# A fused kernel whose engines follow a planned order: weight blocks of 1024 columns, a backward run that hands out banks, and one more unit turned by TensorE

## The chip, the cores and the metric

The kernel runs on one core of one Trainium2 chip. The metric is device time in microseconds (us), the median of several executions of the same program. TensorE (PE) does the matrix products, VectorE (DVE) and ScalarE (ACT) the elementwise work, GpSimd (POOL) almost nothing here, and SyncE (SP) issues every DMA from one queue in program order.

## The reference, cut to what matters

```python
# attention: q, k, v, a_re, a_im of shape (4, 8, 768, 48); a normalised to at most 0.999 in size
for t in range(S):
    new_re = ar * S_re - ai * S_im
    new_im = ar * S_im + ai * S_re
    S_re, S_im = new_re + k[t] (x) v[t], new_im
    y[:, :, t] = q[t] . S_re
x = y.transpose(0, 2, 1, 3).reshape(3072, 384)
h = x @ w_in                                    # layer 1: 384 -> 2048
g = 0 if h <= -1, h if h >= 1, else (h + 1) ** 2 / 4
x = g @ w_out                                   # 2048 -> 384
x = x / sqrt(mean(x * x) + 1e-6) * rms_g        # layer 2
out = (silu(x @ w_gate) * (x @ w_val)) @ w_out2 # 384 -> 1536 -> 384
```

The weights lie in DRAM as 64-bit floats.

## The kernel before, in words

**Units.** The work is cut into 12 units: 2 pairs of batches times 6 chunks of 128 time steps, so that a unit is 256 tokens. A unit goes through attention (`attn`), layer 1 (`moe1`) and layer 2 (`moe2`). Units 0 and 1 go through layer 1 in two halves of 128 tokens.

**Attention of a unit.** A long chain on DVE (tiles X, pr, C, K, E) multiplies up the decays. At its end the real part is X minus the part `a<-X,E`. Either DVE subtracts (`X<-a`, called the fold here), or, for a unit in `PEW['add']`, TensorE adds the two while it transposes (`onto_tokens`). The decays then scale q and k on the token side (`factors`). q and k are split into two f16 parts (`qhi`, `qlo`, `khi`, `klo`), and each part is transposed by a DMA, or for a unit in `PEW['t']` by products with `nid` (minus the identity) that ACT takes out of PSUM (`turned`, L738). For a unit in `PEW['k']` the low part of k comes from a product on TensorE instead of a DVE subtraction (`low_pe`, L747). For a unit in `PEW['n']` TensorE also turns the normalised tokens between the layers (`xnh`, `xnl` from tiles `nh`, `nl`).

**Weights.** `split_w` (L772) loads a block of 64-bit weights, DVE rebuilds an f32 word by one TENSOR_SCALAR and two SCALAR_TENSOR_TENSOR (tile `wv` for layer 1, `spt` for gate and value), ACT writes the f16 high part, and TensorE and ACT make the low part in pieces of 384 columns (two products and one ACT copy each). The blocks of `w_in` and `w_out` pass through slots cut out of tiles that layer 2 fills later (`ring1` for the loads, `ringc` for the words). All weights then stay on the chip.

**The order.** No loop sets the order of the instructions. All operations are recorded, class `Plan` makes a list schedule from a table of costs (`order`), and the program is issued in that order from one line (`issue`), so every row of the trace has line L456. The priority of an operation is its `late`, the latest time by a backward run (`latest`) through the schedule before, plus a shift that the table `SHIFT` gives for its stage. Attention of the next units is recorded between the steps of the layers at `RATES`. `bank` (6 PSUM banks) and `tmp` (4 tiles) are handed out while `order` runs, within the `CAPS` of each kind of user. The backward run does not know of them.

**Stretches.** In the trace before, the first layer-1 product of unit 0 starts at 90.35 us, the first layer-2 (gate) product at 200.77 us, and the first layer-1 product of unit 2 at 296.50 us. From 373 us on the products follow each other almost without a gap, up to 1056.5 us.

Of the kernel before, what the change touches and what calls it, by code (L numbers as in the profile page):

```python
# [48 lines left out]
PEW = {'add': [1], 'sum': [], 'k': [2], 'q': [], 'p': [], 'g': [], 'm': [], 't': [0], 'x': [], 'n': []}  # L49

SHIFT = {'w1a': 12, 'm23': 12, 't40': -12, 'm22': 2, 'w2': 25, 't30': -1, 'c2': 3, 'y21': 5, 'c3': -1}
ORDER = [(1, 0), (1, 1), (2, 0), (2, 1), (1, 2)]
RATES = [14.7, 0, 40.2, 27.7, 29.4]
RATE = 0.62
AHEAD1, STEP1, STEP2 = 4, 5, 6
LAG = 3
CHECKS = 12
# [3 lines left out]
CAPS = {'mo': 4, 'at': 4, 'w': 4, 'n': 2, 'mo_': 3, 'at_': 3, 'w_': 2, 'out_': 1, 'one_': 1}  # L61
ROUNDS = 1
# [20 lines left out]
class Plan:  # L83
# [92 lines left out]
    def add(self, variants):  # L176
# [19 lines left out]
        if "T" in variants:  # L196
            f32 = args[1].dtype == F32
            mm = (300 if name == "transpose" else 6 + n * (4 if f32 else 1), kw_rows(args, kw))
# [56 lines left out]
    def cost(key, name, n, args, kw, ins):  # L255
# [13 lines left out]
        if key == "T":  # L269
            f32 = args[1].dtype == F32  # L270
            return 0.4167e-3 * (300 if name == "transpose" else 6 + n * (4 if f32 else 1))
# [27 lines left out]
    def latest(self, res):  # L299
# [6 lines left out]
        ready = [0.0] * len(ops)  # L306
        free = {k: 0.0 for k in self.engines}
        wait_q = {k: [] for k in self.engines}
        av_q = {k: [] for k in self.engines}
        eng = [next(iter(op.alts)) for op in ops]  # L310
        for op in ops:
            if not left[op.idx]:
                heapq.heappush(wait_q[eng[op.idx]], (0.0, op.idx))
        n = 0
        while n < len(ops):
# [15 lines left out]
            op = ops[heapq.heappop(a)[1]]  # L331
# [4 lines left out]
            op.late = -st  # L336
            for p in op.preds:
# [5 lines left out]
        for op in ops:  # L343
            op.late -= first

# [10 lines left out]
    def order(self):  # L356
# [22 lines left out]
        while len(res) < len(ops):  # L379
# [25 lines left out]
            lack = [v[0] for v in new if not spare[v[0]]] + [v[3] for v in new if turns.get(v[3], 0) != v[4] or using.get(v[3], 0) >= CAPS[v[3]]]  # L405
# [261 lines left out]
def fused_kernel(ctx, tc, q, k, v, a_re, a_im, w_in, w_out, w_gate, w_val, w_out2, rms_g, out, a_ch, qvk_t, given=None):  # L667
# [95 lines left out]
    ring1 = itertools.cycle([flat16(w2)[:, i * 3072:(i + 1) * 3072].bitcast(I64) for i in range(3)])  # L763
    ring12 = itertools.cycle([flat16(w2)[:, i * 3072:(i + 1) * 3072].bitcast(I64) for i in range(2)])
    diag = [flat16(w2)[:, 6144 + i * 256:6400 + i * 256].bitcast(F32) for i in range(KD)]
    ringc = itertools.cycle([flat16(wv)[:, i * 1536:(i + 1) * 1536].bitcast(F32) for i in range(6)])
# [5 lines left out]
    def split_w(src, hi, lo, n, scale, phase, dg=None, part=""):  # L772
# [18 lines left out]
        for c0 in range(0, n, 384):  # L791
            sl = slice(c0, min(n, c0 + 384))
# [11 lines left out]
    def w_1_steps():  # L804
        for f in range(0, DFF, 512):
            sl = slice(f, min(DFF, f + 512))
            for kc in range(KD):
                split_w(w_in[kc * P:(kc + 1) * P, sl], wi_h[:, kc, sl], wi_l[:, kc, sl], sl.stop - f, SW, 1, part="abcd"[f // 512])
                yield
            for j in range(f // P, f // P + 4, 2):  # L810
# [640 lines left out]
```

## Time and profile before

| | us |
|---|---|
| median of 3 executions | 1066.04 (1065.69 to 1067.02) |
| profiled execution, its own time | 1067.5 |
| its span in the profile | 1065.8 |
| PE busy | 995.5 |
| DVE busy | 817.2 |
| ACT busy | 812.7 |

The profile shows one execution. Its span starts with the first and ends with the last instruction, and lies 1.7 us under that execution's own time. An engine counts as busy while at least one of its instructions runs, and the granted clock is the share of its full speed that TensorE was given.

### The profile page before, as it was taken

The numbers are of one execution on the slowest core, as the hardware profiler recorded it, in microseconds if no ns is written. First come the engines' busy times: TensorE is split into PE (matmuls) and PEld (weight loads), VectorE is DVE, ScalarE is ACT, GpSimd is POOL, SyncE is SP. The second block draws the span as 40 slices with busy tenths as digits, with TensorE's granted clock in tenths as the row PEclk, the third lists the DMA queues.
The fourth block names the chain that finished last, engine by engine and source line by source line (L and its number), as shares of the span: only waits on it lengthen the run. The fifth ranks groups of instructions, "written<-read, shape, count | busy, mean of one in ns | idle before, by whom it ended". The sixth has DMA issues, their size and how long they took to land.

```text
span 1065.8 us, 23000 instructions
## 1 busy us (share of the span) xinstructions
PE 995.5 (93%) x9224; PEld 775.2 (73%) x9224; DVE 817.2 (77%) x1721; ACT 812.7 (76%) x1585; POOL 16.7 (2%) x27
## 2 busy tenths in 40 slices
PE   3577998998997899999999999999999999999996
PEld 1355866876875688778777787787887787877874
DVE  9989889979869889698797697896996984633321
ACT  6469879867787798899877897978978989946221
POOL 2000000000000000000000000000000000000000
PEclk9878998999998999999999999999999999999999
DMA  7563265256444443444335526336444321210000
GB/s 255 193 208 121 48 192 138 73 148 159 130 105 123 118 126 94 138 107 105 103 90 147 141 62 168 84 102 169 108 132 139 78 73 36 48 24 16 16 9 26
DMA packets 156018, 115.87 MB, mean 109 GB/s; under 512 B 135296, under 2 KB 138368, under 8 KB 155904
## 3 DMA queue, kind: packets, MB, share of 16 engines
q1 hardware_dynamic: 155904, 114.33, 40.0%
q8 instruction: 74, 1.21, 0.4%
q14 instruction: 40, 0.33, 0.1%
HBM read 77.07 MB, written 4.72 MB: 77 GB/s over the span
## 4 chain that ended last, share of the span: by engine, by line
PE 68%; DVE 16%; ACT 7%; DMA 4%; issue 4%; POOL 0%; SPq 0%; DVEq 0%; ACTq 0%
PE bank L456 43%; PE acc L456 25%; DVE tmp L456 3%; DVE X L456 3%; DVE pr L456 2%; ACT tmp L456 2%; DVE wv L456 2%; DMA w<-in_moe_w_out_dram 1%; ACT L456 1%; DMA spt<-in_moe_w_in_dram 1%; DVE gml L456 1%; DMA qvk<-in_qvk_t_dram 1%; ACT S L456 1%; DVE a L456 1%; ACT X L456 1%
## 5 line engine op out<-in xcount | busy, mean ns | idle before, releaser
L456 DVE SCALAR_TENSOR_TENSOR tmp<-bank,tmp 128x512 f32<-128x512 f32 (+1 forms) x184 | 117.0, 639 | 102.9 <-ACT tmp L456 56.2
L456 PEld LDWEIGHTS <-gmh 128*128 128x128 f16 x1344 | 130.1, 98 | 76.4 <-issue 10.6
L456 PE MATMUL bank<-xTh,wi_h 128*128 128x256 f16 (+1 forms) x672 | 169.1, 262 | 5.2 <-DVE S L456 2.6
L456 PE MATMUL bank<-xTl,wi_h 128*128 128x256 f16 (+1 forms) x672 | 169.0, 262 | 0.3 <-DMA xTl<-nl 0.3
L456 PE MATMUL bank<-xTh,wi_l 128*128 128x256 f16 (+1 forms) x672 | 169.0, 262 | 0.0
L456 ACT ACTIVATE gmh<-tmp 128x512 f16<-128x512 f32 (+1 forms) x184 | 107.5, 588 | 64.7 <-DVE tmp L456 50.4
L456 PE MATMUL bank<-xnh,wv 128*128 128x256 f16 x864 | 155.2, 273 | 0.0
L456 PEld LDWEIGHTS <-wi_h 128*128 128x128 f16 x1344 | 127.2, 100 | 27.1 <-issue 5.8
L456 PE MATMUL acc<-w,gmh 128*128 128x384 f16 x576 | 140.6, 326 | 1.9 <-DVE nl L456 0.7
L456 PEld LDWEIGHTS <-wv 128*128 128x128 f16 x1296 | 126.5, 98 | 16.7 <-issue 0.7
L456 PE MATMUL acc<-wo_h,gmh 128*128 128x384 f16 x384 | 126.5, 329 | 3.6 <-ACT tmp L456 3.6
L456 PE MATMUL acc<-wo_h,gml 128*128 128x384 f16 x384 | 126.3, 329 | 1.8 <-DVE gml L456 1.8
L456 PE MATMUL acc<-wo_l,gmh 128*128 128x384 f16 x384 | 126.5, 329 | 0.0
L456 ACT ACTIVATE tmp<-tmp 128x512 f32<-128x512 f32 (+1 forms) x224 | 124.7, 565 | 2.1
L456 PE MATMUL bank<-xnl,wv 128*128 128x256 f16 x432 | 117.7, 273 | 0.0
L456 PE MATMUL bank<-xnh,wg_l 128*128 128x256 f16 x432 | 117.7, 273 | 0.0
L456 PE MATMUL bank<-xnl,wg_h 128*128 128x256 f16 x432 | 117.7, 273 | 0.0
L456 PE MATMUL bank<-xnh,wg_h 128*128 128x256 f16 x432 | 117.7, 273 | 0.0
L456 PEld LDWEIGHTS <-gml 128*128 128x128 f16 x672 | 66.0, 98 | 47.5 <-DVE gml L456 2.6
L456 PEld LDWEIGHTS <-wg_h 128*128 128x128 f16 x864 | 84.1, 98 | 16.1 <-issue 1.1
L456 PE MATMUL acc<-w,gml 128*128 128x384 f16 x288 | 93.9, 326 | 0.0
L456 ACT ACT_TABLE_LOAD x67 | 86.0, 1283 | 4.9 <-DMA spt<-in_moe_w_in_dram 3.0
(185 smaller groups left out, 2192.1 us busy)
## 6 DMA issues: line engine op xcount, KB each, us to landing
qvk<-in_qvk_t_dram SPq DMA_DIRECT2D x24, 576.0 KB
spt<-in_moe_w_out_dram SPq DMA_DIRECT2D x14, 768.0 KB
a<-in_a_ch_dram SPq DMA_DIRECT2D x12, 768.0 KB
w<-in_moe_w_in_dram SPq DMA_DIRECT2D x12, 512.0 KB
w<-in_moe_w_out_dram SPq DMA_DIRECT2D x8, 768.0 KB
w<-in_moe_w_gate_dram SPq DMA_DIRECT2D x6, 768.0 KB
w<-in_moe_w_val_dram SPq DMA_DIRECT2D x6, 768.0 KB
spt<-in_moe_w_out_dram SPq DMA_DIRECT2D x12, 384.0 KB
```

Of the source, the lines that this page charges most:

```text
L456: getattr(self.engines[k], name)(*args, **kw)
```

## The change

Five things change together.

- `w_in` is loaded and decoded in blocks of 1024 columns instead of 512, so there are 6 loads of 1 MB instead of 12 of 512 KB. A slot grows with them: `ring1` has 2 slots instead of 3, `ringc` 4 instead of 6. The pieces for the low part are 512 columns wide where the block allows it.
- The backward run `latest` hands out banks and tiles too, within the same caps, and the two runs are repeated up to 10 times (`ROUNDS`) instead of once.
- `PEW`: unit 1's fold goes from TensorE to DVE (`'add'`), the low part of unit 2's k from TensorE to DVE (`'k'`), unit 1's q and k are turned by TensorE and not by DMA (`'t'`), and so are the normalised tokens of unit 0 (`'n'`).
- The tables that set priorities and the pace of the side work are new: `SHIFT` has 43 entries instead of 9, and `RATES`, `RATE`, `STEP2`, `CHECKS` and `CAPS` differ.
- The planner's price of a transpose rises from 300 to 320 columns, and a product costs at least 61.

```diff
-PEW = {'add': [1], 'sum': [], 'k': [2], 'q': [], 'p': [], 'g': [], 'm': [], 't': [0], 'x': [], 'n': []}
-SHIFT = {'w1a': 12, 'm23': 12, 't40': -12, 'm22': 2, 'w2': 25, 't30': -1, 'c2': 3, 'y21': 5, 'c3': -1}
+PEW = {'add': [], 'sum': [], 'k': [], 'q': [], 'p': [], 'g': [], 'm': [], 't': [0, 1], 'x': [], 'n': [0]}
+SHIFT = {'t11': 10, 'c0': -52, 'w1h': 416, 'w1e': 5, 't20': 9, 't10': 19, 't40': -45, 'y10': -108, 't21': -6, 'y20': 4, 'w3c': -46, 'y21': -156, 'y31': -154, 'm13': 61, 'w1a': -33, 't00': -24, 'c1': 9, 'y00': 1, 'y01': -103, 'm20': 3, 't01': -24, 'y11': -35, 'c5': -37, 'w1b': -7, 'c4': 10, 'm10': 7, 'w3a': 8, 'm11': 5, 'c2': -138, 'y40': 44, 'm12': 72, 'y30': 28, 'm21': 27, 'w3b': -61, 'w1g': 137, 'w2': -101, 't41': -178, 'y41': -20, 'w1f': -5, 't31': -12, 'm22': 8, 't30': -2, 'c3': 8, 'w2b': -6}
 ORDER = [(1, 0), (1, 1), (2, 0), (2, 1), (1, 2)]
-RATES = [14.7, 0, 40.2, 27.7, 29.4]
-RATE = 0.62
-AHEAD1, STEP1, STEP2 = 4, 5, 6
+RATES = [11.7, 0, 19.2, 44.7, 47.4]
+RATE = 0.58
+AHEAD1, STEP1, STEP2 = 4, 5, 12
...
-CHECKS = 12
+CHECKS = 10
...
-CAPS = {'mo': 4, 'at': 4, 'w': 4, 'n': 2, 'mo_': 3, 'at_': 3, 'w_': 2, 'out_': 1, 'one_': 1}
-ROUNDS = 1
+CAPS = {'mo': 4, 'at': 4, 'w': 4, 'n': 2, 'mo_': 3, 'at_': 2, 'w_': 1, 'out_': 1, 'one_': 1}
+ROUNDS = 10
 LAT = {'V': 0.13, 'A': 0.145, 'G': 0.1, 'T': 0.0, 'S': 0.0}
 XLAT = {'V': 0.13, 'A': 0.145, 'G': 0.1, 'T': 0.2, 'S': 0.0}
...
         mm = None
         if "T" in variants:
...
-            mm = (300 if name == "transpose" else 6 + n * (4 if f32 else 1), kw_rows(args, kw))
+            mm = (320 if name == "transpose" else max(61, 6 + n * (4 if f32 else 1)), kw_rows(args, kw))
...
             return 0.06 + n * {"tensor_tensor": 2.12e-3, "scalar_tensor_tensor": 3.75e-3, "memset": 1.1e-3}.get(name, 3.6e-3)
         if key == "T":
...
-            return 0.4167e-3 * (300 if name == "transpose" else 6 + n * (4 if f32 else 1))
+            return 0.4167e-3 * (320 if name == "transpose" else max(61, 6 + n * (4 if f32 else 1)))
         return 1.25 if "transpose" in name else 0.4
...
             prio[i] = t + ops[i].alts[k]
         left = [len(op.succs) for op in ops]
         ready = [0.0] * len(ops)
+        eng = [next(iter(op.alts)) for op in ops]
         free = {k: 0.0 for k in self.engines}
         wait_q = {k: [] for k in self.engines}
         av_q = {k: [] for k in self.engines}
-        eng = [next(iter(op.alts)) for op in ops]
+        users, spare, held, stuck, turns, using = {}, {}, set(), {}, {}, {}
         for op in ops:
+            for v in op.tiles:
+                users[v] = users.get(v, 0) + 1
+                spare.setdefault(v[0], [0.0] * v[2])
+                turns[v[3]] = max(turns.get(v[3], 0), v[4])
             if not left[op.idx]:
                 heapq.heappush(wait_q[eng[op.idx]], (0.0, op.idx))
         n = 0
...
                 heapq.heappush(a, (-prio[i], i))
             if not a:
                 continue
-            op = ops[heapq.heappop(a)[1]]
+            i = heapq.heappop(a)[1]
+            op = ops[i]
+            new = [v for v in op.tiles if v not in held]
+            lack = self.lacking(new, spare, turns, using)
+            if lack:
+                stuck.setdefault(lack[0], []).append(i)
+                continue
+            when = max([spare[v[0]][0] for v in new], default=0.0)
+            if when > t + 1e-9:
+                heapq.heappush(w, (when, i))
+                continue
+            for v in new:
+                held.add(v)
+                heapq.heappop(spare[v[0]])
+                turns[v[3]], using[v[3]] = v[4] - 1, using.get(v[3], 0) + 1
+                for j in stuck.pop(v[3], ()):
+                    heapq.heappush(wait_q[eng[j]], (max(ready[j], t), j))
             n += 1
             c = op.alts[k]
             st = t + (op.dma + 2.0 if op.dma else 0.0) + c
             free[k] = t + max(op.dma, c) if op.dma else st
             op.late = -st
+            for v in op.tiles:
+                users[v] -= 1
+                if not users[v]:
+                    heapq.heappush(spare[v[0]], st + XLAT[k])
+                    using[v[3]] -= 1
+                    for j in stuck.pop(v[0], []) + stuck.pop(v[3], []):
+                        heapq.heappush(wait_q[eng[j]], (max(ready[j], st + XLAT[k]), j))
             for p in op.preds:
                 ready[p] = max(ready[p], st + (LAT[eng[p]] if eng[p] == k else XLAT[eng[p]]))
                 left[p] -= 1
...
         first = min(op.late for op in ops)
         for op in ops:
             op.late -= first
+    @staticmethod
+    def lacking(new, spare, turns, using):
+        return ([v[0] for v in new if not spare[v[0]]] +
+                [v[3] for v in new if turns.get(v[3], 0) != v[4] or using.get(v[3], 0) >= CAPS[v[3]]])
...
                 late, i = heapq.heappop(a)
             op = ops[i]
             new = [v for v in op.tiles if v not in held]
-            lack = [v[0] for v in new if not spare[v[0]]] + [v[3] for v in new if turns.get(v[3], 0) != v[4] or using.get(v[3], 0) >= CAPS[v[3]]]
+            lack = self.lacking(new, spare, turns, using)
             if lack:
                 stuck.setdefault(lack[0], []).append(i)
                 continue
...
     flat16 = lambda t: t.rearrange("p two a b -> p (two a b)")
-    ring1 = itertools.cycle([flat16(w2)[:, i * 3072:(i + 1) * 3072].bitcast(I64) for i in range(3)])
+    ring1 = itertools.cycle([flat16(w2)[:, i * 4096:(i + 1) * 4096].bitcast(I64) for i in range(2)])
     ring12 = itertools.cycle([flat16(w2)[:, i * 3072:(i + 1) * 3072].bitcast(I64) for i in range(2)])
...
-    ringc = itertools.cycle([flat16(wv)[:, i * 1536:(i + 1) * 1536].bitcast(F32) for i in range(6)])
+    ringc = itertools.cycle([flat16(wv)[:, i * 2048:(i + 1) * 2048].bitcast(F32) for i in range(4)])
     spt = plan.tile(mp, [P, 768], I64, "spt")
...
         flat = lambda t: t.rearrange("p a b -> p (a b)") if len(t.shape) > 2 else t
         hf, lf = flat(hi), flat(lo)
-        for c0 in range(0, n, 384):
-            sl = slice(c0, min(n, c0 + 384))
+        step = 512 if n % 512 == 0 else 384
+        for c0 in range(0, n, step):
+            sl = slice(c0, min(n, c0 + step))
             w = sl.stop - c0
             lp = bank("w")[:, 0:w]
             with plan.group():
...
         return src[j * P:(j + n) * P, :].rearrange("(a p) c -> p a c", p=P)
     def w_1_steps():
-        for f in range(0, DFF, 512):
-            sl = slice(f, min(DFF, f + 512))
+        for f in range(0, DFF, 1024):
+            sl = slice(f, f + 1024)
             for kc in range(KD):
-                split_w(w_in[kc * P:(kc + 1) * P, sl], wi_h[:, kc, sl], wi_l[:, kc, sl], sl.stop - f, SW, 1, part="abcd"[f // 512])
+                split_w(w_in[kc * P:(kc + 1) * P, sl], wi_h[:, kc, sl], wi_l[:, kc, sl], sl.stop - f, SW, 1, part="ab"[f // 1024])
                 yield
-            for j in range(f // P, f // P + 4, 2):
-                split_w(rows(w_out, j, 2), wo_h[:, j:j + 2, :], wo_l[:, j:j + 2, :], 2 * DM, SW, 1, part="efgh"[f // 512])
+            for j in range(f // P, f // P + 8, 2):
+                split_w(rows(w_out, j, 2), wo_h[:, j:j + 2, :], wo_l[:, j:j + 2, :], 2 * DM, SW, 1, part="efgh"[j // 4])
                 yield
...
```

Counted over the whole program, TensorE gains 64 products that turn q and k and 12 that turn `nh` and `nl`, and loses the 12 products of the fold with `a` (its 12 with `X` become plain transposes), the products for unit 2's k, and some of the pieces of weights. On DVE 18 instructions of `wv` go (TENSOR_SCALAR 20 to 14, SCALAR_TENSOR_TENSOR 40 to 28), `a<-X,E` goes from 23 to 24, `X<-a` from 22 to 24, `klo` from 22 to 24, and the one `X<-X,E` goes. ACT gains 16 copies of turned q and k and 4 of turned tokens and loses 6 of high parts and 12 of low parts of weights and 4 of `klo`; its table loads go from 67 to 71. SP issues 306 DMAs instead of 324.

**The start of SP's queue.** `w_0` is the slot tile of the weights, `a_0` the decays, `qvk` the tokens. Before, the program begins:

```order
L456 DMA a_0_104<-in_a_ch_dram 128x1536
L456 DMA w_0_74<-in_moe_w_in_dram 128x512 x2
L456 DMA qvk_113<-in_qvk_t_dram 128x1152
L456 DMA w_0_74<-in_moe_w_in_dram 128x512
L456 DMA qvk_114<-in_qvk_t_dram 128x1152
L456 DMA g_s_75<-in_moe_rms_g_dram 128x3x1
L456 DMA w_0_74<-in_moe_w_out_dram 128x2x384 x2
L456 DMA w_0_74<-in_moe_w_in_dram 128x512 x2
L456 DMA w_0_74<-in_moe_w_out_dram 128x2x384
```

With the change:

```order
L490 DMA a_0_104<-in_a_ch_dram 128x1536
L490 DMA w_0_74<-in_moe_w_in_dram 128x1024 x2
L490 DMA qvk_113<-in_qvk_t_dram 128x1152
L490 DMA qvk_114<-in_qvk_t_dram 128x1152
L490 DMA g_s_75<-in_moe_rms_g_dram 128x3x1
L490 DMA w_0_74<-in_moe_w_in_dram 128x1024
L490 DMA w_0_74<-in_moe_w_out_dram 128x2x384 x4
L490 DMA w_0_74<-in_moe_w_in_dram 128x1024 x3
```

Two large loads now stand where three smaller ones stood before a slot is used again, and the third load of `w_in` is the first that has to wait for a slot.

**PE where unit 1's fold is.** `idt` is the identity, `xTh` and `wi_h`, `wi_l` are layer 1's tokens and weights of unit 0, `gmh` and `wo_h` the second product of layer 1. Before:

```order
L456 MATMUL bank_119<-xTh_99,wi_l_68 128x128
L456 MATMUL bank_103<-idt_81,X_105 128x128 x6
L456 MATMUL bank_122<-idt_81,a_0_104 128x128 x6
L456 LDWEIGHTS gmh_154
L456 MATMUL acc_0_158<-wo_h_69,gmh_154 128x384
```

With the change:

```order
L490 MATMUL bank_119<-xTh_99,wi_l_68 128x128
L490 MATMUL bank_123<-spt_92,w_0_74 128x384
L490 LDWEIGHTS nid_80
L490 MATMUL bank_123<-wv_73,nid_80 128x384
L490 MATMUL bank_115<-idt_81,X_105 128x128 x3
L490 MATMUL bank_116<-idt_81,X_105 128x128 x3
L490 LDWEIGHTS wi_h_67
```

Twelve products with `X` and `a` became six plain transposes of `X` alone, and a piece of the gate weights (`spt`) now stands ahead of them.

**DVE where the gate and value weights are decoded.** `spt` holds the decoded word, one TENSOR_SCALAR and two SCALAR_TENSOR_TENSOR to a block. Before, the eleventh of the 12 blocks stands amid the norm of unit 0 (`y_1`) and unit 2's chain (X, pr):

```order
L456 TENSOR_TENSOR y_1_165<-y_1_164 128x1
L456 TENSOR_TENSOR X_105<-pr_106 128x2x96
L456 TENSOR_TENSOR y_1_165<-y_1_165,ms_163 128x1
L456 TENSOR_SCALAR spt_92<-w_0_74 128x768
L456 TENSOR_SCALAR y_1_165<-y_1_165 128x1
L456 TENSOR_TENSOR pr_106<-X_105 128x384
L456 TENSOR_TENSOR y_1_165<-y_1_165,y_1_164 128x1
L456 SCALAR_TENSOR_TENSOR spt_92<-w_0_74,spt_92 128x768
```

With the change it stands amid the masks of unit 1's scores (`tmp<-bank,maskt`) and some 80 rows earlier:

```order
L490 TENSOR_TENSOR pl_127<-tmp_148,ph_126 128x512
L490 TENSOR_TENSOR pl_130<-tmp_128,ph_129 128x512
L490 SCALAR_TENSOR_TENSOR spt_92<-w_0_74,spt_92 128x768
L490 TENSOR_SCALAR spt_92<-w_0_74 128x768
L490 SCALAR_TENSOR_TENSOR spt_92<-w_0_74,spt_92 128x768
L490 SCALAR_TENSOR_TENSOR h_0_0_134<-bank_119,h_0_0_134 128x384
L490 TENSOR_SCALAR fx_133<-St_88 128x1
```

In number of instructions the stretch of DVE ahead of the first gate product is nearly unchanged (415 before, 419 after), but it holds more of the long ones: `a<-X,E` 6 instead of 3, `X<-a` 6 instead of 2, no `X<-X,E` instead of 1 (unit 2's fold now stands ahead of the gate product too), a twelfth block of gate and value weights, and two blocks of `w_out2`. Ahead of the first layer-1 product DVE has 151 instructions instead of 169: the 18 of `wv` are gone and the rest is the same.

## Rows read from the trace of the kernel before

**Rows 1.** Page, section 1: busy time, share of the span and instructions of each engine.
```profile
PE 995.5 (93%) x9224; PEld 775.2 (73%) x9224; DVE 817.2 (77%) x1721; ACT 812.7 (76%) x1585; POOL 16.7 (2%) x27
```

**Rows 2.** Stretches: length; busy PE, PEld, DVE, ACT, POOL; granted clock, DMA share, GB/s.
```profile
0.00:90.35 90.35, 50.92 (x245) 30.11 (x245) 83.75 (x172) 56.50 (x119) 6.49 (x13) 0.83 0.61 205
90.35:200.77 110.42, 102.13 (x1144) 82.64 (x1142) 101.07 (x250) 92.60 (x229) 2.21 (x3) 0.95 0.44 117
200.77:296.50 95.73, 92.40 (x815) 70.80 (x813) 82.46 (x179) 72.49 (x136) 0.79 (x1) 1.00 0.53 139
296.50:373.00 76.50, 67.55 (x618) 49.98 (x616) 60.83 (x126) 58.74 (x116) 0.70 (x1) 0.93 0.45 116
373.00:1056.50 683.50, 682.33 (x6409) 541.57 (x6407) 488.17 (x995) 531.75 (x987) 6.51 (x9) 1.00 0.35 91
```

**Rows 3.** What PE waited for, 201 to 374 us: total, times, longest.
```profile
PE acc L456 <- ACT tmp L456: 4.3, 2, 3.6
PE bank L456 <- DVE X L456: 2.2, 1, 2.2
PE bank L456 <- DVE pl L456: 1.9, 2, 1.2
PE acc L456 <- DVE gml L456: 1.8, 1, 1.8
```

**Rows 4.** DVE groups by form, whole span: count, busy and mean ns, idle before.
```profile
L456 DVE SCALAR_TENSOR_TENSOR wv<-w,wv 128x512 uint32<-128x512 uint32 x24 | 16.5, 689 | 0.0
L456 DVE SCALAR_TENSOR_TENSOR wv<-w,wv 128x768 uint32<-128x768 uint32 x16 | 15.2, 956 | 0.0
L456 DVE TENSOR_TENSOR a<-X,E 128x1536 f32<-128x1536 f32 x23 | 40.2, 1749 | 0.0
L456 DVE TENSOR_TENSOR X<-a 128x768 f32<-128x768 f32 x22 | 20.9, 948 | 0.0
```

**Rows 5.** What DVE waited for, 0 to 90.35 us: total, times, longest.
```profile
DVE wv L456 <- DMA w<-in_moe_w_out_dram: 3.5, 2, 2.1
DVE wv L456 <- DMA w<-in_moe_w_in_dram: 0.6, 1, 0.6
```

**Rows 6.** Chain that ended last, two loads on it: start, length, what.
```profile
40.65 6.56 DMA w<-in_moe_w_out_dram
64.20 7.74 DMA w<-in_moe_w_out_dram
```

**Rows 7.** PE in order of time, unit 1's fold on TensorE, one batch.
```profile
119.49 2.91 PE L456 MATMUL bank<-idt,X 128*128 128x128 f32 x12
...
124.91 0.33 PE L456 MATMUL acc<-wo_h,gmh 128*128 128x384 f16 x1
```

**Rows 8.** PE in order of time, six plain transposes (unit 0) and what follows.
```profile
78.86 1.06 PE L456 MATMUL bank<-idt,X 128*128 128x128 f32 x6
79.76 0.19 PE L456 MATMUL bank<-vh,ph 128*128 128x48 f16 x1
```

**Rows 9.** PE in order of time, low part of unit 2's k, one batch.
```profile
217.40 0.81 PE L456 MATMUL bank<-S,idt 128*128 128x384 f32 x2
...
219.02 0.27 PE L456 MATMUL bank<-xnh,wg_h 128*128 128x256 f16 x1
```

**Rows 10.** PE in order of time, eight turns of unit 0 and what follows.
```profile
95.79 0.65 PE L456 MATMUL bank<-nid,klo 128*96 128x128 f16 x8 [0.55 <-DVE klo L456]
96.27 0.22 PE L456 MATMUL bank<-xTh,wi_h 128*128 128x128 f16 x1
```

**Rows 11.** ACT groups by form, whole span.
```profile
L456 ACT ACT_TABLE_LOAD x67 | 86.0, 1283 | 4.9 <-DMA spt<-in_moe_w_in_dram 3.0 <-PEq L1423 0.8
L456 ACT ACTIVATE khT<-bank 96x512 f16<-96x512 f32 x4 | 2.1, 580 | 0.0
```

**Rows 12.** ACT in order of time, around one table load.
```profile
209.35 1.28 ACT L456 ACT_TABLE_LOAD   x1
210.65 0.62 ACT L456 ACTIVATE S<-S,e 128x384 f32<-128x384 f32 x1
```

## The prediction, made before the changed kernel had run

> **What bounds the kernel now.** I read the busy shares first. PE is busy 995.5 us, DVE 817.2 and ACT 812.7 [rows 1], which says that PE leads and not where. So I cut the span into stretches at PE's own milestones [rows 2]. From 373 to 1056.5 us PE is busy 682.33 of 683.50 us at the full clock, 2.4 GHz: there only PE's own work counts, and what DVE, ACT or a DMA do is hidden. Before 90 us PE is busy 50.92 of 90.35 us and DVE 83.75: the start is DVE's. From 90 to 201 us DVE is busy 101.07 of 110.42, PE 102.13 and ACT 92.60: all three are nearly full, and DVE has the chains that the others wait for. From 201 to 373 us PE is busy 92.40 + 67.55 of 172.23 us, so 12.3 us idle, and the granted clock of the second half is 0.93. At 1.2 GHz a product takes twice as long, so (1 - 0.93) x 76.5 = 5.4 us is the most that the lower clock can have cost there. Then I asked what PE waited for in that stretch [rows 3]: ACT's `tmp` 4.3 us, and DVE's `X`, `pl` and `gml` 2.2 + 1.9 + 1.8 = 5.9 us. The 9.3 us from 1056.5 to the end of the span stay as they are, since the same instructions end both programs.
>
> The time is thus the moment at which the first gate product can start (200.8 us), plus the PE work that is left then, plus the stalls among it, plus the tail. I cost the change in these four parts.
>
> **The start, up to the first layer-1 product: -1 us.** The list of DVE instructions ahead of it is the same but for 18 fewer of `wv`. A SCALAR_TENSOR_TENSOR takes 689 ns at 512 columns and 956 at 768 [rows 4], so 256 columns more cost 267 ns and 1024 columns some 1223 (an estimate from these two). Two blocks of 512 at 689 cost 1378, so each pair that is merged saves 155 ns, and 18 merged pairs, the TENSOR_SCALAR put in at the same price, 2.8 us at most. At least it is nothing, if DVE then waits for something else. I take 1.5. Against it stands the smaller number of slots. DVE waits 3.5 + 0.6 = 4.1 us for weights now [rows 5]. Two loads of `w_out` on the critical chain took 6.56 and 7.74 us of 768 KB [rows 6], a mean of 7.2; scaled by bytes, 1 MB would take 9.5 (an estimate; with two in flight instead of three it may be less). With the decode behind it, about 3 us for a block of 1024 and 2.5 for one of 768, a slot turns in 12.5 or 9.7 us. Two slots have 6 large and 8 small loads to turn: (6 x 12.5 + 8 x 9.7) / 2 = 76 us of the 90. They fit, though with only 14 us over, where three slots had far more. Bounds: the 4.1 us go altogether, or each of the 12 loads that use a slot again is late by 1 us more, +12. I take +0.5, nearer the low end because of the 14 us over.
>
> **From there to the first gate product: +9 us.** The new order brings more DVE work ahead of it in nearly the same number of instructions. The folds: 3 more `a<-X,E` at 1749 ns and 4 more `X<-a` at 948, less one `X<-X,E`, priced like `a<-X,E`: 5.2 + 3.8 - 1.7 = 7.3 us. The twelfth gate and value block and two blocks of `w_out2`, three instructions each: at 956 ns for 768 columns and 555 for 384 (by the slope of the two forms) 2.9 + 2 x 1.7 = 6.2 at most, and I take 5, because the TENSOR_SCALAR reads one operand less. Nine small steps of attention more (`qvk`, `vl`, `S`, `qlo`, `hl`, `E`) of 384 columns mostly: half the 948 ns of a 768-column step each, +4. A few steps of layer 1 fewer: -1.5. Together +15. DVE is idle for 110.42 - 101.07 = 9.3 us of this stretch. If the new work fills all of that, the gate product comes +6 later; if none, +15. I take +9, since PE's and ACT's results, for which DVE waits now, come no sooner. PE itself has no more to do ahead of that product: its list loses 9 us of fold and gains 4.5 of turns and 6 of weight pieces, with 1.5 less of layer 1. ACT gets 16 more copies at 580 ns, 9.3 us [rows 11], in part instead of copies that go, and 4 more table loads.
>
> **PE's work behind the gate product: -8 us.** Unit 1's fold on TensorE took 124.91 - 119.49 = 5.42 us for one batch [rows 7]. Six plain transposes took 79.76 - 78.86 = 0.90 [rows 8]. For two batches 2 x (5.42 - 0.90) = -9.0. Unit 2's `klo` took 219.02 - 217.40 = 1.62 us a batch [rows 9]: -3.2. The 64 new turns go at the pace of the eight that took 96.27 - 95.79 = 0.48 us [rows 10]: 64 x 0.06 = +3.8; the 12 for `nh` and `nl` likewise +0.7. The sum is -7.7 us of PE work over the whole program, and as the work ahead of the gate product is equal within a us, all of it shows behind. In the span's last 683 us such work is paid one to one, so I keep -8 with bounds of 1 us to either side.
>
> **Stalls between 201 and 373 us: -10 us.** 12.3 us of idle PE, and up to 5.4 of clock, can be given back at most, nothing at least. DVE enters this stretch some 14 us ahead (the folds and the last weight block are done), which is what the 5.9 us of waits for DVE's `X`, `pl` and `gml` want [rows 3]; they sit in layer 1 and attention of units 1 and 2. The 4.3 us for ACT's `tmp` are one long wait of 3.6 us and may stay or go. I take 5.9 + 2 + half of the clock's 5.4 = 10.6, and round down to 10. The clock would follow because it was at the full level wherever PE stood without gaps, in the stretch from 373 us on, and at 0.93 to 0.95 where it had gaps [rows 2].
>
> **Cost put at nothing.** DVE has 2 folds' steps and 2 `klo` more, and ACT 20 more copies: they lie beside PE's work from 201 us on, where DVE is idle 29 of 172 us and ACT 41 [rows 2]; uncovered, DVE's part would be 1.7 + 2 x 0.9 + 2 x 0.9 - 1.7 = 3.8 us and ACT's 20 x 0.58 = 11.6. Eight fewer DMA transposes for unit 1 and four for unit 0 free SP's queue, and no wait of PE between 201 and 373 us is for a DMA [rows 3]. ACT's 4 more table loads are 4 x 1283 ns = 5.1 us [rows 11], and the next instruction starts 0.02 us after one [rows 12]. The Trainium skill, page "ScalarE: Activation LUTs", section "What ACT_TABLE_LOAD costs", adds a drain of some 1380 ns to each switch; by it the four would cost 10.6 us, which this trace contradicts with its 0.02 us.
>
> **The sum.** 1065.8 - 1 + 9 - 8 - 10 = 1055.8 us of span. The profiled execution's own time lies 1.7 us above its span and 1.5 above the median of the runs shown, so the median is 0.2 above the span: 1056.0.
>
> **Rivals.**
>
> - *DVE's early work is paid in full and the stalls stay* (slower). The gate product comes +15 later, DVE stays behind, and unit 1's and 2's chains give PE the same 12.3 us of gaps: 1065.8 - 1 + 15 - 8 = 1071.8. For it speaks that three engines are nearly full from 90 to 201 us. Against it: the work is moved, not added, so DVE has less to do afterwards. It decides where the stretch from the first layer-1 product to the gate product grows beyond 120 us while PE still idles 12 us up to the solid stretch. Chance 0.20.
> - *Only a trade* (same). DVE's +15 is paid, and the stalls on DVE, 5.9 us, go: 1065.8 - 1 + 15 - 8 - 5.9 = 1065.9. Chance 0.10.
> - *Two slots are too few.* Each reuse waits 1 us more, +12 in the start, the rest as forecast: about 1067. For it speaks that SP's queue issues in order, so a load that waits for a slot also holds up the decays and tokens of unit 1 behind it; against it the 14 us over. Chance 0.07.
> - *Better.* The early DVE work fits into the waits (+6), and nearly all stalls and the low clock go (-17): 1065.8 - 1 + 6 - 8 - 17 = 1045.8. This is what a backward run that knows of the banks would give if the gaps are waits for banks: PE waits then because a bank's user came too early. Chance 0.20.
> - *ACT becomes the bound* from 90 to 201 us: 92.60 busy of 110.42, and 16 copies with 4 loads are 9.3 + 5.1 = 14.4 us more if none of the dropped copies lies there, so 107: it just fits in 119. About 1067. Chance 0.03.
>
> **How the numbers follow.** The forecast holds 0.40, which makes it the likeliest case; its own range is 1043 to 1066, from its bounds (-4 to +6 around the start's and the gate's terms, -7 to +8 on the stalls) added as if independent. The bound between a change and none is 0.2%, about 2 us and about what a measurement of this kernel can tell (its three runs span 0.12%). Faster, under 1063.9: 0.36 of the forecast's 0.40, the better case's 0.20, 0.03 of the trade and 0.03 of slots and ACT together: 0.62. Within 0.2%: 0.06 of the trade and 0.03 each of the forecast and of slots and ACT: 0.12. Slower: the first rival's 0.20, 0.04 of slots and ACT, and 0.01 each of trade and forecast: 0.26. The range reaches from 1042, some 4 us below the better case, to 1074, 2 above the slower one; outside lie the farthest parts of these two and of an unforeseen kind, under 2 in 10.
>
> **What would show it.** Right: the first layer-1 product at 88 to 92 us; 118 to 121 us from it to the first gate product, DVE busy there for over 112; PE busy 988 us in all; idle PE under 5 us between the gate product and the solid stretch, with the waits for `X`, `pl` and `gml` gone; the granted clock 0.97 or more there. Wrong: DVE waiting over 10 us for `w` in the start, a gate product after 212 us with as many gaps behind it, or PE gaps appearing in the solid stretch, where SHIFT and RATES alone decide when the next units' attention runs.

## The result, and the profile after

The changed kernel takes 1052.61 us (median of 4, 1051.82 to 1054.27) against 1065.87 for the kernel before in the same comparison: a ratio of 0.9877, 95% interval 0.9860 to 0.9894, so 13 us or 1.2% faster. 1056.0 had been forecast. The profiled execution has a span of 1050.9 us and took 1052.71.

The busy time of the engines in the page of the profile, beside [rows 1]:

```profile
PE 983.3 (94%) x9216; PEld 761.3 (72%) x9216; DVE 817.2 (78%) x1707; ACT 823.0 (78%) x1587; POOL 18.7 (2%) x27
```

The stretches of the changed kernel, cut at the same products as [rows 2] (first layer-1 product of unit 0 at 92.36, first gate product at 203.07; the cut at 296 is only near the one of before); columns as there:

```profile
0.00:92.36 92.36, 52.55 (x222) 26.24 (x223) 87.69 (x160) 59.21 (x106) 6.49 (x13) 0.84 0.64 211
92.36:203.07 110.71, 100.80 (x1182) 78.26 (x1181) 108.93 (x262) 100.99 (x251) 2.48 (x2) 0.96 0.34 108
203.07:296.00 92.93, 92.79 (x872) 72.72 (x870) 79.12 (x172) 63.78 (x125) 1.10 (x2) 1.00 0.44 110
296.00:373.00 77.00, 70.39 (x732) 55.18 (x731) 64.91 (x135) 64.07 (x127) 0.70 (x1) 0.98 0.47 104
373.00:1041.60 668.60, 666.24 (x6219) 528.79 (x6217) 475.69 (x978) 534.36 (x980) 7.99 (x9) 1.00 0.38 95
```

Three things are to be seen against [rows 2]. First, the gate product comes only 2.3 us later (203.07 for 200.77), although DVE has done more by then: two more rows, of each kernel from its start to its gate product, first before and then changed:

```profile
0.00:200.77 200.77, 153.05 (x1387) 112.75 (x1387) 184.82 (x421) 149.10 (x347) 8.70 (x16) 0.90 0.51 157
```

```profile
0.00:203.07 203.07, 153.35 (x1402) 104.50 (x1403) 196.62 (x421) 160.20 (x356) 8.97 (x15) 0.91 0.47 155
```

PE did the same work (153.05 and 153.35), DVE 196.62 - 184.82 = 11.8 us more, and DVE's idle time went from 16.0 to 6.5. Second, the time from the gate product to 373 us has 0.14 + 6.61 = 6.8 us of idle PE where there were 12.3, and in the later of its two stretches a clock of 0.98 where it was 0.93. Third, the time from the gate product to the last product is 1041.6 - 203.07 = 838.5 us instead of 855.7.

What PE waited for from 203 to 374 us, the rows that are read below, beside [rows 3]:

```profile
PE bank L490 <- DVE S L490: 3.0, 1, 3.0
PE acc L490 <- DVE nl L490: 1.0, 1, 1.0
PE bank L490 <- DVE pl L490: 1.0, 1, 1.0
PE acc L490 <- DVE gml L490: 0.6, 1, 0.6
PE bank L490 <- DVE X L490: 0.2, 1, 0.2
```

The long wait for ACT's `tmp` (4.3 us) is gone, that for `X` fell from 2.2 to 0.2, `pl` and `gml` are smaller, and one of 3.0 us for `S` is new. All that DVE waited for a DMA in the start, beside [rows 5], is now a gate block, and no layer-1 weights:

```profile
DVE spt L490 <- DMA w<-in_moe_w_gate_dram: 1.6, 1, 1.6
```

The decode by form, beside [rows 4]. A block of 1024 columns takes 1220 ns, where 1223 had been estimated from the two shorter forms:

```profile
L490 DVE SCALAR_TENSOR_TENSOR wv<-w,wv 128x1024 uint32<-128x1024 uint32 x12 | 14.6, 1220 | 0.0
```

ACT's table loads, beside [rows 11], and one load in order of time:

```profile
L490 ACT ACT_TABLE_LOAD x71 | 91.1, 1283 | 2.5 <-PEq L1458 0.8 <-PE bank L490 0.2
```

```profile
207.62 1.28 ACT L490 ACT_TABLE_LOAD   x1
208.92 0.60 ACT L490 ACTIVATE tmp<-bank 128x512 f32<-128x512 f32 x1
```

The four more loads cost 91.1 - 86.0 = 5.1 us, and the next instruction starts 0.02 us after the load. By the Trainium skill, page "ScalarE: Activation LUTs", section "What ACT_TABLE_LOAD costs", some 1380 ns of drain would come on top of each; this trace, like [rows 12], has no such gap behind the load, and none ahead of it (the instruction before ends at 207.61).

### The profile page after: what moved, and what is told of

The parts are those of the page before. It is cut to its first block, busy times and chain, and to the rows that moved or that the text cites. A ratio compares the mean times of both kernels' runs of the same rounds, so it can differ in the third digit from the quotient of the medians.

```text
span 1050.9 us, 22946 instructions
## 1 busy us (share of the span) xinstructions
PE 983.3 (94%) x9216; PEld 761.3 (72%) x9216; DVE 817.2 (78%) x1707; ACT 823.0 (78%) x1587; POOL 18.7 (2%) x27
## 4 chain that ended last, share of the span: by engine, by line
PE 68%; DVE 22%; ACT 6%; issue 3%; POOL 0%; DVEq 0%; ACTq 0%; POOLq 0%
PE bank L490 42%; PE acc L490 26%; DVE X L490 3%; DVE wv L490 3%; DVE tmp L490 3%; DVE pr L490 2%; DVE a L490 2%; DVE spt L490 2%; DVE gml L490 1%; DVE S L490 1%; ACT tmp L490 1%; ACT X L490 1%; DVE qvk L490 1%; ACT S L490 1%; DVE pl L490 1%
## 5 line engine op out<-in xcount | busy, mean ns | idle before, releaser
L490 PE MATMUL bank<-xTh,wi_h 128*128 128x256 f16 (+1 forms) x672 | 166.9, 260 | 8.4 <-DVE S L490 3.0
L490 PE MATMUL bank<-xTh,wi_l 128*128 128x256 f16 (+1 forms) x672 | 166.8, 260 | 0.0
L490 PEld LDWEIGHTS <-wg_h 128*128 128x128 f16 x864 | 84.1, 98 | 14.9 <-issue 0.4
L490 ACT ACT_TABLE_LOAD x71 | 91.1, 1283 | 2.5 <-PEq L1458 0.8
```

Source lines behind the costliest of these rows:

```text
L490: getattr(self.engines[k], name)(*args, **kw)
```

## The experiments

Twelve kernels ran, in four groups. Theory A is the prediction's: the work that goes from PE is paid, and the order, with DVE further ahead, closes the gaps. The rivals stand with each.

**One part undone, the rest as changed.** The planner makes a new order each time.

`a_pew`, the old choice of what TensorE does:

```diff
-PEW = {'add': [], 'sum': [], 'k': [], 'q': [], 'p': [], 'g': [], 'm': [], 't': [0, 1], 'x': [], 'n': [0]}
+PEW = {'add': [1], 'sum': [], 'k': [2], 'q': [], 'p': [], 'g': [], 'm': [], 't': [0], 'x': [], 'n': []}
```

> The changed kernel with PEW of before (unit 1's fold and unit 2's low part of k on TensorE again, unit 1's q and k turned by DMA, unit 0's normalised tokens too); all else as changed, planned anew. Theory A (the prediction's: PE's work is paid one to one wherever it lies, and the order removed the stalls): 7.7 us of PE work come back, so 1052.6 + 8 = 1060, between 1058 and 1063, with the gaps behind the first gate product still small. Rival B (PE's work in the stretch from the first layer-1 to the first gate product is hidden beside DVE): only the 3.2 us of unit 2's k are paid, 1055 to 1057. Rival C (who does the fold, the turns and the k decides the stalls): over 1064.

`a_blocks`, blocks of 512 columns:

```diff
-    ring1 = itertools.cycle([flat16(w2)[:, i * 4096:(i + 1) * 4096].bitcast(I64) for i in range(2)])
+    ring1 = itertools.cycle([flat16(w2)[:, i * 3072:(i + 1) * 3072].bitcast(I64) for i in range(3)])
...
-        for f in range(0, DFF, 1024):
+        for f in range(0, DFF, 512):
...
```

> The changed kernel with blocks of 512 columns, three slots of load and six of words again. Theory A (the start saves little by the blocks): 1 to 3 us slower, 1053.6 to 1055.6, with DVE's waits for weights near the 4.1 us of before. Rival B (larger blocks are what lets DVE run ahead and fills its idle time up to the gate product): 6 us slower or more. Rival C (three slots are better, as the two cost waits on SP's queue): faster than 1052.

`a_back`, the old `latest` and one round:

```diff
-ROUNDS = 10
+ROUNDS = 1
...
-            lack = self.lacking(new, spare, turns, using)
-            if lack:
-                stuck.setdefault(lack[0], []).append(i)
-                continue
...
```

> The changed kernel with the backward run of before (which hands out no banks) and one round; tables and all else as changed. Theory A (the order removed the stalls, by the backward run and the tables together): the 9 us of gaps and low clock behind the gate product come back in part, 1056 to 1063. Rival B (the tables alone set the order): within 2 us of 1052.6. Rival C (the tables only fit this backward run): over 1066, worse than before the change.

`a_tab`, the old tables (`CHECKS` and `CAPS` too, which the cut leaves out):

```diff
-RATES = [11.7, 0, 19.2, 44.7, 47.4]
-RATE = 0.58
-AHEAD1, STEP1, STEP2 = 4, 5, 12
+RATES = [14.7, 0, 40.2, 27.7, 29.4]
+RATE = 0.62
+AHEAD1, STEP1, STEP2 = 4, 5, 6
...
+SHIFT = {'w1a': 12, 'm23': 12, 't40': -12, 'm22': 2, 'w2': 25, 't30': -1, 'c2': 3, 'y21': 5, 'c3': -1}
...
```

> The changed kernel with SHIFT, RATES, RATE, STEP2, CHECKS and CAPS of before; backward run, blocks and PEW as changed. Theory A (backward run and tables each bring a part of the 9 us): 1055 to 1060, with the first gate product later than 205 us or gaps of over 8 us behind it. Rival B (the tables alone set the order): 1062 or more. Rival C (the backward run alone does it): within 2 us of 1052.6.

**One part alone, put into the kernel before.** The edits are those of the change, one at a time, each shown by a line or two. The fifth part, the planner's prices of a transpose and of a short product, was neither undone nor put in alone:

```diff
+PEW = {'add': [], 'sum': [], 'k': [], 'q': [], 'p': [], 'g': [], 'm': [], 't': [0, 1], 'x': [], 'n': [0]}
```

> The kernel before with the new PEW alone. Theory A (PE's work is paid one to one wherever it lies): 7.7 us less, 1058, between 1056 and 1060. Rival B (hidden beside DVE up to the gate product; DVE gets the fold and the low part of k on top): 1063 to 1068.

```diff
...
+        for f in range(0, DFF, 1024):
...
```

> The kernel before with blocks of 1024 columns, two slots of load and four of words alone. Theory A: 1 to 3 us less, 1063 to 1065. Rival B (the blocks let DVE run ahead): 1060 or less. Rival C (two slots make DVE wait): over 1067.

```diff
+ROUNDS = 10
...
+            lack = self.lacking(new, spare, turns, using)
...
```

> The kernel before with the new backward run, which hands out banks and tiles, and up to ten rounds, alone. Theory A (it brings a part of the 9 us of stalls): 1058 to 1063. Rival B (the tables alone set the order): 1064 to 1068. Rival C (the old tables don't fit it): over 1070.

```diff
...
+RATES = [11.7, 0, 19.2, 44.7, 47.4]
+RATE = 0.58
...
```

> The kernel before with the new SHIFT, RATES, RATE, STEP2, CHECKS and CAPS alone. Theory A (they bring a part of the 9 us): 1058 to 1063. Rival B (the tables alone set the order): 1057 or less. Rival C (the new tables only fit the new backward run): over 1068.

What came out. The ratio is to the kernel before; the gate column is the start of the first gate product; the two idle columns are PE's idle time in the 172 us behind it (for the first two kernels up to 373 us), and from there to the last product, worked out from the windows of each profile.

| kernel | median us | ratio, 95% interval | gate, us | idle in 172 us | idle later |
|---|---|---|---|---|---|
| before | 1065.9 to 1067.5 | 1 | 200.8 | 12.3 | 1.2 |
| changed | 1052.61 | 0.9877 (0.9860 to 0.9894) | 203.1 | 6.8 | 2.4 |
| `a_pew` | 1085.24 | 1.0169 (1.0155 to 1.0183) | 221.0 | 12.6 | 7.8 |
| `a_blocks` | 1097.37 | 1.0282 (1.0264 to 1.0300) | 219.8 | 16.9 | 11.3 |
| `a_back` | 1089.65 | 1.0206 (1.0188 to 1.0224) | 211.6 | 20.7 | 6.5 |
| `a_tab` | 1084.01 | 1.0150 (1.0132 to 1.0169) | 205.9 | 27.3 | 1.5 |
| `b_pew` | 1081.82 | 1.0132 (1.0117 to 1.0148) | 198.8 | 11.9 | 16.1 |
| `b_blocks` | 1093.69 | 1.0240 (1.0226 to 1.0254) | 206.6 | 11.9 | 16.0 |
| `b_back` | 1068.86 | 1.0015 (1.0006 to 1.0024) | 211.6 | 11.4 | 0.1 |
| `b_tab` | 1108.73 | 1.0377 (1.0363 to 1.0391) | 210.7 | 15.6 | 19.7 |

Each of the four parts alone makes the kernel slower, by 1.4 to 41 us, and each of them taken back makes it slower than both, by 29 to 43 us against the changed kernel (by the two ratios). None of theory A's eight numbers held. In number, though not in what they gave as the reason, rival C fits `a_pew`, `a_back`, `b_blocks` and `b_tab`, and rival B `a_blocks` and `a_tab`; `b_back` lies next to rival B, and `b_pew` is beyond both. The losses don't lie in the part: with the old `PEW`, by the prediction's prices 7.7 us of PE work come back, but the kernel loses 31. And `b_pew` has its gate product 2 us earlier than before and then loses 16.1 us of idle PE behind 371 us, where the kernel before has 1.2. The stretch that counted as solid is solid only in an order that fits it. What PE waited for there in `b_pew`, the four longest:

```profile
PE bank L456 <- DMA xTh<-nh: 4.8, 2, 4.2
PE bank L456 <- DVE nl L456: 4.2, 3, 2.9
PE bank L456 <- DVE X L456: 1.7, 1, 1.7
PE bank L456 <- DVE S L456: 1.5, 1, 1.5
```

These are steps of the next units' attention (`X`, `S`) and the tokens between the stages (`nh`, `nl`), which come late in its order. So these eight can't price a part. They price a part plus a new order made with tables that do not belong to it.

**The order moved alone.** `a_nudge` changes one number of `SHIFT` by 1:

```diff
-'t10': 19,
+'t10': 20,
```

> The changed kernel with one of the 43 entries of SHIFT changed by 1 ('t10' from 19 to 20), planned anew: a fifth of PE's rows then stand elsewhere. Theory A (the gain is that of one order among many, which the tables pick; the parts alone lost 1 to 41 us because the old tables pick a poor order for them): 3 to 20 us slower. Rival B (the order is good because of the backward run and the parts, the tables need not be exact): within 3 us of 1052.6.

It took 1093.76 us, ratio 1.0242 (1.0223 to 1.0262): by the two ratios, 1.0242 / 0.9877 = 1.037, some 39 us more than the changed kernel, with the same work to do (9216 instructions of PE and 1707 of DVE in both). Rival B is out, and the loss is larger than theory A's own 3 to 20. Its windows behind the first gate product (at 207.0) show where:

```profile
207.00:297.00 90.00, 90.00 (x836) 70.61 (x834) 74.64 (x160) 63.48 (x119) 0.55 (x1) 1.00 0.41 109
297.00:379.00 82.00, 70.23 (x667) 53.61 (x665) 63.04 (x129) 62.01 (x122) 1.27 (x1) 0.94 0.42 108
379.00:1082.70 703.70, 677.20 (x6320) 537.55 (x6317) 480.65 (x987) 530.91 (x983) 7.21 (x9) 0.98 0.36 89
```

703.70 - 677.20 = 26.5 us of idle PE stand in the long stretch, and one wait makes up 16.2 of them. What PE waited for from 385 to 500 us, the two longest:

```profile
PE bank L490 <- DMA khT<-khi: 16.2, 1, 16.2
PE bank L490 <- DVE X L490: 5.3, 1, 5.3
```

SP's queue at that place, in order of time:

```profile
413.81 1.29 SPq L490 DMA_TRANSPOSE qlT<-qlo  x1
421.76 0.34 SPq L490 DMA_DIRECT2D qvk<-in_qvk_t_dram  x1
423.09 0.38 SPq L490 DMA_DIRECT2D spt<-in_moe_w_out_dram  x1
423.82 1.42 SPq L490 DMA_TRANSPOSE khT<-khi  x1
425.29 5.24 SPq L490 DMA_TRANSPOSE klT<-klo  x1
```

ACT's step that makes `khi`, the piece of the chain of waits that follows, and PE's first product behind the wait:

```profile
422.97 0.82 ACT L490 ACTIVATE khi<-S 128x768 f16<-128x768 f32 x1
```

```profile
423.09 7.50 DMA spt<-in_moe_w_out_dram
430.67 1.37 ACT spt L490 x4
```

```profile
431.69 0.29 PE L490 MATMUL bank<-qhT,khT 96*128 96x128 f16 x1 [16.20 <-DMA khT<-khi]
```

The wait begins at 431.69 - 16.20 = 415.49 and has two halves. PE came to the scores of a unit before ACT had made `khi` (423.79): 8.3 us. Then the transpose, issued at once (423.82), stood 0.7 us behind a load of 768 KB, of weights that are read again only for a check at the end, and PE went on at 431.69, a us after that load had ended (430.59): 7.9 us. So an order that brings ACT's step late and one load early costs 16 us at one place. That it was this load that held the transpose up is read from times, here and in other runs (last section); a run without the load was not made.

**Work added in a fixed order.** The last three keep the order as it is and repeat instructions that write the same values again, so what they cost is the price of that work at that place.

```diff
             for _, i, k in self.given.res:
                 for name, args, kw in self.ops[i].calls[k]:
-                    getattr(self.engines[k], name)(*args, **kw)
+                    again = 6 if name == "transpose" and self.ops[i].stage in ("t10", "t11") else 1
+                    for _ in range(again):
+                        getattr(self.engines[k], name)(*args, **kw)
```

> The changed kernel in its own order, nothing planned anew, but each of the 12 plain transposes of unit 1's X issued six times: 60 transposes more at 0.15 us, 9.0 us of TensorE at the place where the fold was. Theory A (the prediction's term: PE's work of the fold is paid one to one, whether its place is DVE's stretch or not): 1052.6 + 9 = 1061.6, between 1060 and 1063. Rival B (in the stretch up to the first gate product PE waits for DVE anyway, and the fold on TensorE was hidden): 1052 to 1056, with the first gate product hardly later.

It took 1058.76 us, ratio 0.9924 (0.9909 to 0.9938). By the two ratios to the kernel before, 0.9924 / 0.9877 = 1.0048: 5 us more than the changed kernel, give or take 2.4 (the two intervals' halves, 0.0015 and 0.0017, taken together). That lies between the two theories, and the gate product comes 5.6 us later, against rival B. Its stretch to the gate product, beside the row of the changed kernel above:

```profile
91.90:208.70 116.80, 109.91 (x1244) 87.26 (x1243) 109.21 (x262) 101.21 (x251) 2.48 (x2) 0.96 0.32 102
```

PE is busy 109.91 - 100.80 = 9.1 us more and the stretch is 6.1 longer; PE's idle time in it fell from 9.9 to 6.9. In this profile a third of the work fell into gaps and two thirds were paid. The time from the gate product to the last product is the same to 0.1 us (838.4 and 838.5).

```diff
+            nv = 0
...
                     getattr(self.engines[k], name)(*args, **kw)
+                    nv += k == "V"
+                    if k == "V" and name == "tensor_tensor" and 160 < nv < 425:
+                        out, n = args[0].tensor.name, args[0].size() // P
+                        if out.startswith("klo") or out.startswith("pr") and n == 384:
+                            getattr(self.engines[k], name)(*args, **kw)
```

> The changed kernel in its own order, but 14 products of X in the attention chain (551 ns each) and three low parts of k (949 ns) between the first layer-1 product and the first gate product are issued twice: 10.5 us more for VectorE there. Theory A (DVE is full in that stretch, 108.9 of 110.7 us, so it is paid almost in full): 1061 to 1064, with the gate product 8 to 10 us later. Rival B (PE has enough other work ahead, so DVE's time there is hidden): under 1057.

It took 1064.29 us, ratio 0.9976 (0.9966 to 0.9986). 0.9976 / 0.9877 = 1.0100, so 10.6 us more than the changed kernel, give or take 2.1: the 10.5 us in full, as theory A says, though its median lies just above theory A's range. The gate product stands at 215.1, 12 us later, where 8 to 10 had been expected.

The same in the kernel before, with 170 in place of 160:

> The kernel before in its own order with the same 17 instructions issued twice, 10.5 us more for VectorE between its first layer-1 product and its first gate product, where it was idle for 9.3 us. Theory A (the prediction's: new DVE work falls partly into the idle time; the measured change says that nearly all does): 1067 to 1072, with DVE's idle time in that stretch down to under 4 us. Rival B (the idle time is waiting for PE and ACT and doesn't take work): 1075 to 1078.

It took 1077.17 us, ratio 1.0096 (1.0081 to 1.0112): 10.2 us more, paid in full there too, with the median as in rival B. Its stretch from the first layer-1 product:

```profile
88.90:208.70 119.80, 104.50 (x1144) 83.80 (x1143) 110.65 (x266) 91.93 (x228) 2.21 (x3) 0.92 0.40 108
```

DVE's idle time is still 9.2 us. What it waited for in the kernel before, in `b_dve10` and in the changed kernel, the first rows of each over the same stretch:

```profile
DVE qvk L456 <- ACT S L456: 4.6, 3, 1.7
DVE tmp L456 <- PE bank L456: 1.5, 1, 1.5
DVE qvk L456 <- PE bank L456: 1.2, 1, 1.2
```

```profile
DVE qvk L457 <- ACT S L457: 4.6, 3, 1.7
DVE qvk L457 <- PE bank L457: 1.2, 1, 1.2
```

```profile
DVE qlo L490 <- ACT qhi L490: 0.7, 1, 0.7
DVE tmp L490 <- ACT tmp L490: 0.4, 1, 0.4
```

The three waits for ACT's `S` stand at 4.6 us in the kernel before and in `b_dve10`, although DVE does 110.65 - 101.07 = 9.6 us more in the latter: none of the repeats stands right ahead of one of the three waiting instructions. What fills such a wait is seen at unit 1's second batch. DVE in order of time, first before and then changed:

```profile
151.72 0.61 DVE L456 SCALAR_TENSOR_TENSOR qvk<-qvk,fl,bank 128x384 f32<-128x384 f32 x1 [1.72 <-ACT S L456]
152.25 0.61 DVE L456 SCALAR_TENSOR_TENSOR nl<-bank,fx,nh 128x384 f16<-128x384 f32 x1
154.39 0.61 DVE L456 SCALAR_TENSOR_TENSOR qvk<-qvk,fl,bank 128x384 f32<-128x384 f32 x1 [1.53 <-ACT S L456]
```

```profile
151.47 0.60 DVE L490 SCALAR_TENSOR_TENSOR qvk<-qvk,fl,bank 128x384 f32<-128x384 f32 x1
151.99 0.95 DVE L490 SCALAR_TENSOR_TENSOR spt<-w,spt 128x768 uint32<-128x768 uint32 x1
152.86 0.95 DVE L490 TENSOR_TENSOR X<-X 128x768 f32<-128x768 f32 x1
153.73 0.61 DVE L490 SCALAR_TENSOR_TENSOR nl<-bank,fx,nh 128x384 f16<-128x384 f32 x1
154.25 0.54 DVE L490 TENSOR_TENSOR hl<-h,hh 128x384 f16<-128x384 f32 x1
154.72 0.60 DVE L490 SCALAR_TENSOR_TENSOR qvk<-qvk,fl,bank 128x384 f32<-128x384 f32 x1
```

Between the two `qvk` one instruction stood, and DVE idled 1.53 us. Now four stand there, a step of a gate block and one of `X` among them, and DVE does not wait. A run with repeats at such a place was not made.

## Why the prediction was right, and where it was not

**The direction and the size.** 13 us faster were measured and 10 forecast, the time is 3.4 us under the forecast and inside its own narrow range of 1043 to 1066. Of the span: the start +2.0 (forecast -1), the stretch to the gate product +0.3 (+9), and from there to the last product -17.2 (-18), together -14.9 where -10 had been forecast. So the part behind the gate product was forecast to 0.8 us, while of the two terms ahead of it one was 3.0 too low and the other 8.7 too high. That they cancel in part is luck. The range itself was added up wrongly: its bounds, taken as independent, give 8 us down and 10 up, 1048 to 1066 and not from 1043. The measured time lies in both.

Of the signs listed for being right, the granted clock came out (0.98 and more). The first layer-1 product (92.36 us) lies just beyond 88 to 92. The stretch behind it took 110.7 us and not 118 to 121, DVE was busy 108.9 us there and not over 112, PE was busy 983.3 us in all and not 988, and PE's idle time behind the gate product was 6.8 us and not under 5.

**PE's work behind the gate product, -8: right.** PE's busy time there fell from 842.3 to 829.4 us, 12.9. The lower clock explains at most 5.4 - 1.5 = 3.8 of it, worked out as in the prediction from the clocks of the fourth stretch, so 9.1 or more are work. `a_fold9` qualifies the price of the fold: at its own place two thirds of it cost time. It came out whole because the new order put other PE work (the weight pieces) where the fold had been, and so took it out of the time behind the gate product. PE's busy time up to the gate product is the same to 0.3 us, as the order rows had shown. The `spt` products behind the gate product of the kernel before (its groups by form from 200.77 to 1056.5 us), where the changed kernel has none:

```profile
L456 PE MATMUL bank<-spt,w 128*128 128x384 f32 x12 | 4.9, 486 | 0.0
```

**Stalls, -10: right in kind, somewhat large.** Idle PE from the gate product to the last product went from 13.46 to 9.11 us (-4.35), and the clock gave at most 3.8: -8.1. The waits for `X`, `pl` and `gml` shrank from 5.9 to 1.8, as had been said of them, and `tmp` went altogether; a wait of 3.0 for `S` that had not been foreseen came in.

**"From there to the first gate product: +9": the mis-sized step.** The sum of new work was nearly right: DVE did 11.8 us more before the gate product, where 15 less the 1.5 of larger blocks had been counted. Wrong was the sentence that this would be paid for the most part because "PE's and ACT's results, for which DVE waits now, come no sooner". Of DVE's 16.0 us of idle time up to the gate product 9.5 were filled, and the floor of +6 was too high as well, because it counted the 9.3 us of the second stretch and not the 6.6 of the start. By stretches, 3.9 of the 11.8 us were done before the first layer-1 product and only 7.9 behind it, where DVE's idle time fell from 9.3 to 1.8: of this term's +15, 7.9 came and 7.6 of them fell into waits. `a_dve10` and `b_dve10` show that idle time alone is not room: work added in a fixed order, away from the waits, is paid in full in both kernels, in the one before even with 9 us of idle DVE beside it. The rows of unit 1's second batch show what is room: the instructions that the new order puts ahead of the waiting one. That this holds for all of the 7.6 us is read from the three waits for `S` that are gone, and not shown one by one. The order of DVE around each `qvk<-S`, which was at hand before the run, could have told it.

**The start, -1: wrong by 3 us.** The loads did as forecast: DVE's 4.1 us of waiting for weights went, the two slots turn all 14 loads, and the rival of too few slots is out. But in PE's order the turns of unit 0's k now stand ahead of the first layer-1 product, and they wait for ACT:

```profile
91.48 1.09 PE L490 MATMUL bank<-nid,khi 128*96 128x128 f16 x8 [2.69 <-ACT khi L490]
92.36 0.31 PE L490 MATMUL bank<-xTh,wi_h 128*128 128x128 f16 x1
```

In the kernel before, the same turns stood behind the first products, those of `klo` too ([rows 10], at 95.79):

```profile
94.60 0.65 PE L456 MATMUL bank<-nid,khi 128*96 128x128 f16 x8 [0.73 <-ACT khi L456]
```

ACT's `khi` waits for DVE's `S` in its turn, and DVE does 87.69 - 83.75 = 3.9 us more in the start than before, with six of a gate block's longer steps (`spt<-w,spt`) instead of three. The forecast had counted the list ahead of the first layer-1 product and not what DVE does beside it. How much of the 3 us each of the two makes up was not run.

**The rivals.** The slower one needed a stretch of over 120 us with 12 us of idle PE after it; they were 110.7 and 6.8. Its first half is real all the same: `a_dve10` adds such work on purpose, its stretch takes 122.7 us, and it is paid in full, though PE's idle time in the 172 us behind the gate product stays at 6.6. A mere trade is out as well, since the gate product came 2.3 us later and not 15. The better case was halfway true: the early work fitted in still more than it had supposed, and the stalls went only in part. ACT is busy 101 of 110.7 us in the stretch up to the gate product and DVE waits for it little over 1 us there, so it did not become the bound.

**What stays open.** The gain belongs to the set, as one order. Which of the five parts it needs can't be told from runs in which the tables are made for another set, and the planner's prices were not varied at all. `a_nudge` shows that the order alone, with the work unchanged, is worth 39 us. Whether other tables for the kernel before would do as well was not tried.

## What to carry to other kernels

Where a planner sets the order, a change of one number can outweigh the work that the change adds or removes, so forecast from the new order's rows and the old trace's durations, and not from what a part is meant for. A part taken out or put in alone measures the part and an order that nobody chose; to price work, keep the order fixed and repeat the work in place. Idle time of a full engine is a list of places: look at what stands ahead of the waiting instruction in the new order before counting it as room.

## What the runs showed of the hardware that was not expected

A DMA transpose issued 0.7 us behind a load of 768 KB on the same queue let PE go on only 7.9 us after its issue (`a_nudge`, 423.82 to 431.69), 1.1 us after that load had ended. In `a_tab` PE waits for the same kind of transpose, and the last load ahead of it was issued 8.1 us earlier (361.48). PE goes on 3.3 us after its issue:

```profile
369.62 1.23 SPq L490 DMA_TRANSPOSE khT<-khi  x1
372.96 0.29 PE L490 MATMUL bank<-qhT,khT 96*128 96x128 f16 x1 [11.65 <-DMA khT<-khi]
```

The smaller transposes of `nh` show the same: 2.4 us from issue to PE with the last load 6.9 us earlier (`b_pew`, 572.81 to 575.21), 4.6 and 6.0 us with a load of 768 KB 0.4 us earlier (`a_pew`, 363.90 to 368.47, and `a_blocks`, 594.40 to 600.40). In the changed kernel no transpose of k makes PE wait behind the gate product.
